# Relative-position bias of an attention layer: from mirrored distances in DRAM to full rows written into SBUF

## The chip, the cores and the metric

The kernel runs on one core of a Trainium2 chip. The metric is the device time of one execution in microseconds (us). TensorE's engines are called PE (matmuls) and PEld (weight loads), VectorE is DVE, ScalarE is ACT, GpSimd is POOL, and SP issues the DMAs.

## The reference

An attention layer, a dense feed-forward layer and a soft mixture of eight experts follow one another. Only the first is touched:

```python
B, H, S, D = q.shape                                   # 4, 8, 576, 64
scores = scale * np.matmul(q, k.transpose(0, 1, 3, 2))
psi_rel = np.log1p(np.abs(pos[:, None] - pos[None, :]))
psi_i = np.log1p(np.maximum(pos[:, None], 1.0))
x = (psi_rel / psi_i)[..., None]                       # one number per (query, key)
h = np.maximum(x @ w1 + b1, 0.0)                       # 32 hidden units
bias = h @ w2                                          # one bias per head
scores = scores + bias.transpose(2, 0, 1)[None]        # the same for the four batches
attn = softmax(scores); out = attn @ v
```

For a given query the bias is a function of the distance |i - j| alone. A hidden unit is on or off on either side of one distance, since x grows with the distance. So the bias of a pair is x times a sum of w1 w2 over the units that are on, plus a sum of b1 w2 over the same units; the units that are on are a mask of zeros and ones.

## The kernel before

**Bias phase** (`bias_phase`, lines 74 to 261). A mask tile holds 128 rows, 4 keys (distances) times 32 hidden units, and one column per query. `make_mask` (line 139) makes mask t of 144 by comparing the queries' positions `pr` with a threshold `wl` per row, on DVE, POOL or ACT as the table ENGS says (ACT as a very steep sigmoid). Sixteen masks are a key group k, of 64 distances; there are nine. Since only distances are needed, and query i has none beyond max(i, 575 - i), queries are paired from the middle outwards (ROWS, line 1249): the masks of group k have min(576, 128 (9 - k)) columns. `unit(k, c)` (line 153) takes 128 of these columns, as the weights of 48 matmuls of 64 moving columns (line 165): three bf16 parts of the products w1 w2 and b1 w2 for eight heads. There are 30 such units, and five of 64 columns for the middle queries (c = 4), taken two and two. DVE then multiplies by x (line 189) and adds (line 190) into `rows`; POOL writes the same values backwards beside them (line 198). When a chunk of distances is complete, `flush` writes it to the DRAM tensor W (line 203), in which each query has a row of 1152 with the distances to the left and to the right.

**Attention** (class `Attention`, from line 264). 16 pairs of (two heads, batch) have 9 steps each, 144 steps; a step is 128 queries of one head (one step of the nine: the last 64 of both), in the order SLOT. `scores` makes the products in PSUM, `shift` (line 397) adds the bias from the tile `nb` and takes the row's extreme, giving `z`; `weights` (line 416) takes the exponential, `transposes` and `gather` (lines 433, 457) turn it, `pv` (line 472) multiplies by v. The bias of two heads, 128 x 9 x 576 f32, is read from W by `bias_rows` (line 310) with a shifted start in every row, just before the first of the four batches that use it. `split` (lines 345, 348) divides q and k into two parts on POOL. The results go to DRAM as `xT` and `rs` and come back for the feed-forward layer. While the attention runs, DVE also puts together the first weights of the next layer (`half_piece`, lines 641 to 644, from the tile `early`, loaded at line 622).

**Order.** The instructions of each engine are ordered by a planner that simulates the kernel; those that the code marks with `keep_in_program_order` (the attention from pair 1 on, `half_piece`, some DMAs) stay in the order of the code. Each engine takes its instructions strictly in that order; all DMAs of this phase go through SP's queue. PSUM has four accumulators for the bias phase; the attention's tiles take their place. Tiles in SBUF are laid out in stacks from both ends; a tile that lies where an earlier one lay waits until that one has been read for the last time.

Of the kernel before, what the change touches and what calls it, by code (L numbers as in the profile page):

```python
# [35 lines left out]
NG = 9  # L36
NTQ = S // 4
PITCH = 2 * S
RING = 40
ACC = 4  # L40
CHUNKS = ((0, 2, 4, 7, 9), (0, 2, 4, 6, 8), (0, 3, 5, 7), (0, 2, 4, 6), (0, 2, 4, 5))
TAGS = ("cfgc", "becb", "gbd", "ada", "mnm")
LATE, EARLY = "bcdg", "aefmn"
ENGS = (
    "VVVVAAVVVVAVVVVV", "VPAVAVAAAAAAAAVV", "PAAVAVPAAAAAAAVA", "AAAAVVAVVPAAAAAA", "AAAAPAAVPVAPPVAV", "AVAAAPAVAAAVPPAV",
    "AAAAAVVVAAPAAAAA", "PPAAVVAAAVPAVAAA", "APAPPVPVAAAPAAVA",
)
# [26 lines left out]
def bias_phase(tc, ident, W, cpack, lcol, prow, xmain, xtail, att):  # L74
# [3 lines left out]
    with ExitStack() as ctx:  # L78
# [4 lines left out]
        fps = {tag: p for p, tags in ((pool("b_late"), LATE), (pool("b_rows"), EARLY)) for tag in tags}  # L83
        cp = pool("b_const")
        mp = pool("b_mask")
        ap_ = ctx.enter_context(tc.tile_pool(name="b_acc", bufs=ACC, space=PSUM, reuse_waits="tile"))
# [3 lines left out]
        wl = cp.tile([P, NTQ], F32, name="wl")  # L90
        nc.sync.dma_start(wl, lcol)
        pr = cp.tile([P, S], F16, name="pr")
        nc.sync.dma_start(pr, prow)
        xm_t = cp.tile([P, NG, 4, 64], F32, name="xm_t")
        xt_t = cp.tile([P, 3, 64], F32, name="xt_t")
        nc.sync.dma_start(xm_t[:, 0], xmain[:, 0])
# [7 lines left out]
        sg = cp.tile([P, 4], F32, name="sg")  # L104
        nc.scalar.activation(sg[:, 3:4], ident[:, :1], AF.Exp)

# [32 lines left out]
        def make_mask(k, u):  # L139

            t = 16 * k + u
            n = min(S, 128 * (NG - k))
            dst = mask[:, t % RING, :n]
            on = ENGS[k][u]
            if on == "A":
                nc.scalar.activation(dst, pr[:, :n], AF.Sigmoid, bias=wb[:, t : t + 1], scale=BIG)  # L146
            else:
                eng = nc.vector if on == "V" else nc.gpsimd
                eng.tensor_scalar(dst, pr[:, :n], wl[:, t : t + 1], None, ALU.is_gt)

        rows, accs, late = {}, {}, []

        def unit(k, c):

            if c < 4 or k % 2 == 0:
                accs[c] = ap_.tile([P, 2, 2, H, 32], F32, tag="acc", name=f"acc{k}_{c}")
            acc = accs[c]
            if c < 4:
                m, cols, dst = P, slice(P * c, P * c + P), acc
            else:  # L160
                m, cols = 64 * (k % 2) + 64, slice(512, S)
                dst = acc[m - 64 : m]
            for u in range(16):
                for part in range(3):
                    nc.tensor.matmul(  # L165
                        dst[:, u // 8, :, :, 4 * (u % 8) : 4 * (u % 8) + 4],
                        mask[:, (16 * k + u) % RING, cols],
                        wp[:, part],
                        start=part == 0,
                        stop=part == 2,  # L170
                    )
            if c == 4 and k in (0, 2):
                return
            ks = CHUNKS[c]
            i = max(n for n in range(len(ks)) if ks[n] <= k)
            d0, w, f0 = 64 * ks[i], 64 * (ks[i + 1] - ks[i]), 64 * (k - ks[i])
            last = k + 1 == ks[i + 1]
            if c == 4:
                w, f0, xs = 64, 0, xt_t[:m, i]
            else:  # L180
                xs = xm_t[:, k, c]
            if f0 == 0:
                tag = TAGS[c][i]
                rows[c] = fps[tag].tile([P, H, 2 * w], F32, tag=tag, name=f"rows{c}_{i}")
            both = rows[c]
            fwd = both[:m, :, w + f0 : w + f0 + 64]
            tmp = cp.tile([P, 2, H, 32], F32, tag="tmp", name=f"tmp{k}_{c}", bufs=2)
            xb = xs.rearrange("p (s j) -> p s j", s=2).unsqueeze(2).to_broadcast([m, 2, H, 32])
            nc.vector.tensor_tensor(tmp[:m], acc[:m, :, 0], xb, ALU.mult)
            nc.vector.tensor_tensor(fwd.rearrange("p h (s j) -> p s h j", s=2), tmp[:m], acc[:m, :, 1], ALU.add)  # L190

            one = d0 == 0 and c < 4
            z = int(one and f0 == 0)
            a = both[:m, :, w + one - f0 - 64 : w + one - f0 - z]
            back = bass.AP(
                tensor=a.tensor, offset=a.offset + 63 - z, ap=[list(v) for v in a.ap[:2]] + [[-1, 64 - z]]
            )
            nc.gpsimd.tensor_scalar(back, fwd[:, :, z:], 1.0, 1.0, ALU.mult, ALU.mult)
            if not last:
                return  # L200

            def send(dst, src, pin):
                i = nc.sync.dma_start(dst, src)
                if pin:
                    tc.keep_in_program_order(i)

            def put(half, blk, d0, n_r, n_l, one, hs):

                q = slice(64 * half, 64 * half + 64)
                dst = W[blk if blk >= 4 else 3 - blk, hs].rearrange("h p j -> p h j")  # L210
                if one:
                    send(dst[:, :, S - n_l : S - 1 + n_r], both[q, hs, w - n_l + 1 : w + n_r], hs.start > 0)
                    return
                if n_r > 0:
                    send(dst[:, :, S - 1 + d0 : S - 1 + d0 + n_r], both[q, hs, w : w + n_r], hs.start > 0)
                if n_l > 0:
                    y = int(d0 == 0)
                    send(dst[:, :, S - d0 - n_l : S - d0 - y], both[q, hs, w - n_l : w - y], hs.start > 0)

            def flush(hs):  # L220
                if c == 4:
                    for half in range(m // 64):
                        put(half, 4, d0 + 64 * half, 64, 64, False, hs)
                else:
                    far, near = min(w, S - 64 * c - d0), max(0, min(w, 64 * c + 64 - d0))
                    put(0, c, d0, far, near, one, hs)
                    put(1, 8 - c, d0, near, far, one, hs)

            if c < 3 and (k + 1 == ks[-1] or c == 0 and i == 2):
                flush(slice(0, 2))  # L230
                late.append(lambda: flush(slice(2, H)))
            else:
                flush(slice(0, H))
# [3 lines left out]
        nc.sync.dma_start(xt_t, xtail)  # L237
        for k in range(1, NG):
            nc.sync.dma_start(xm_t[:, k], xmain[:, k])
        att.load(0)  # L240
        for k in range(NG):
            cs = [c for c in range(3, -1, -1) if k <= NG - 1 - c]
            if k < 5:
                cs.append(4)
            done = 0
            for n_, c in enumerate(cs):
                unit(k, c)
                if c in (2, 3) and k + c == 8:
                    att.bias_first(3 - c)
                if k + 1 < NG:  # L250
                    upto = 16 * (n_ + 1) // len(cs)
# [3 lines left out]
            if k < 4:  # L255
                att.split(0, k)
        att.load(1)
        att.bias_first(2)
        att.bias_first(3)
        for f in late:  # L260
            f()


class Attention:
# [10 lines left out]
    def __init__(self, tc, ident, W, xT, rs, qk, v_l):  # L275
        self.tc, self.nc, self.ident = tc, tc.nc, ident
        self.W, self.xT, self.rs = W, xT, rs
# [6 lines left out]
    def open_set(self, ctx, n):  # L284
        self.sets[n]["bias"] = ctx.enter_context(self.tc.tile_pool(name=f"a_bias{n}", bufs=1, reuse_waits="tile"))
# [5 lines left out]
    def bias_rows(self, hp, s, n):  # L291

        nb = self.nb[hp]
        nh = 2 if n == 1 else 1
        if s == 4:
# [18 lines left out]
    def bias_first(self, s):  # L314

        if s == 0:
            self.bias_tile(0)
# [1025 lines left out]
```

## Time and profile before

| | |
|---|---|
| time, median of 3 runs | 847.73 us (845.72 to 849.33) |
| profiled execution | 848.92 us |
| its span, first to last instruction | 847.1 us |
| PE, PEld busy | 780.9 us (92%), 641.5 us (76%) |
| DVE, ACT, POOL busy | 565.7 us, 487.7 us, 297.0 us |
| mean granted TensorE clock | 0.967 of full speed |
| HBM read, written | 91.95 MB, 21.29 MB |

The busy time of an engine is the time in which at least one of its instructions runs; matmuls are pipelined, so a busy PE isn't a PE at its peak. The bias phase lasts to about 84 us, the attention to about 323, the rest is the feed-forward layer and the experts. The 40 slices of the profile (21 us each) show PE's granted clock in tenths:

```
PE   6965699999997999999999999999999999998893
DVE  8766468889889885899434756675676556556202
PEclk9988599999999999999999999999999999999898
DMA  6799985845847321455000200230010005338995
```

A row of a view gives the line in the kernel, the engine, the operation and the tiles (written <- read), then the shape and the count. An arrow behind an idle time names what ended it.

### The profile page before, as it was taken

The page shows a single profiled execution, that of the slowest core. Times are in us where ns is not written, and L with a number is a line of the kernel's source. Part 1 is how long each engine was busy: PE and PEld are TensorE (multiplying, and loading weights), DVE is VectorE, ACT ScalarE, POOL GpSimd, SP SyncE. Part 2 cuts the span into 40 slices and gives each one's busy share as a digit, 9 for nine tenths or more (in the row PEclk, how much of TensorE's full clock was granted, in tenths as well). Part 3 has the DMA queues.
Part 4 walks back from the last instruction along what each step waited for, and adds up shares of the span by engine and source line. Part 5 has one row for each costly group of instructions (what it writes and reads, how often), then busy time and mean ns, then how long its engine had stood idle before and what let it go on. Part 6 is the DMA issues. An engine that isn't in the chain of part 4 may idle for free.

```text
span 847.1 us, 18670 instructions
## 1 busy us (share of the span) xinstructions
PE 780.9 (92%) x7444; PEld 641.5 (76%) x7444; DVE 565.7 (67%) x1058; ACT 487.7 (58%) x1066; POOL 297.0 (35%) x285
## 2 busy tenths in 40 slices
PE   6965699999997999999999999999999999998893
PEld 6965577777765776888899889888888898986341
DVE  8766468889889885899434756675676556556202
ACT  8932467787786685443445655656665656565002
POOL 6975143646463420312312241343243232131000
PEclk9988599999999999999999999999999999999898
DMA  6799985845847321455000200230010005338995
GB/s 206 176 224 199 244 199 176 215 156 151 226 126 283 108 71 60 156 199 196 29 1 0 75 1 1 79 112 10 1 29 1 1 14 185 105 119 272 403 369 225
DMA packets 59783, 114.45 MB, mean 135 GB/s; under 512 B 10672, under 2 KB 38192, under 8 KB 57904
## 3 DMA queue, kind: packets, MB, share of 16 engines
q1 hardware_dynamic: 59696, 113.26, 43.8%
q8 instruction: 58, 0.95, 0.5%
q14 instruction: 29, 0.24, 0.1%
HBM read 91.95 MB, written 21.29 MB: 134 GB/s over the span
## 4 chain that ended last, share of the span: by engine, by line
PE 38%; DMA 8%; DVE 2%; ACT 1%; issue 1%; POOL 0%; SPq 0%; DVEq 0%; ACTq 0%
PE ys L723 18%; PE h L690 17%; DMA ep<-in_mw_dram 4%; DMA em<-in_mw_dram 1%; DMA er<-in_mw_dram 1%; DMA rb<-rs 1%; DVE g L701 1%; PE lp L782 1%; DVE vv L604 1%; PE sp L842 0%; PE sp L841 0%; PE tl L829 0%; POOL w79l L679 0%; DMA vv<-xT 0%; DVE emo L1114 0%
## 5 line engine op out<-in xcount | busy, mean ns | idle before, releaser
L701 DVE SCALAR_TENSOR_TENSOR g<-g,nal 128x384 f32<-128x384 f32 x96 | 85.8, 894 | 71.9 <-ACT g L700 71.7
L416 ACT ACTIVATE e<-z,m 128x576 f32<-128x576 f32 x144 | 110.4, 766 | 4.0 <-DVE m L397 3.2
L709 ACT ACTIVATE gr<-g 128x384 fp32r<-128x384 f32 x95 | 49.7, 524 | 106.2 <-DVE g L701 106.2
L397 DVE CUSTOM_DVE_ANT_0 z<-s,nb 128x576 f32<-128x576 f32 x144 | 103.4, 749 | 10.5 <-DMA nb<-W 4.6
L433 PEld LDWEIGHTS t<-ident,e 64*128 64x128 f32 x1440 | 68.3, 143 | 47.4 <-ACT g L457 13.8
L457 ACT ACTIVATE g<-t 128x320 f32<-128x320 f32 x144 | 62.3, 432 | 61.4 <-PE t L433 46.6
L472 PE MATMUL o<-g,v 128*64 128x256 f32 (+1 forms) x640 | 95.2, 420 | 0.0
L433 PE MATMUL t<-ident,e 64*128 64x64 f32 x1440 | 81.4, 233 | 14.7 <-ACT g L457 10.8
L457 DVE COPY g<-t 128x320 f32<-128x320 f32 x144 | 69.4, 486 | 30.8 <-PE t L433 23.6
L165 PE MATMUL acc<-wp,mask 128*128 128x64 bf16 (+1 forms) x1680 | 61.0, 203 | 17.7 <-DVE rows L190 7.0
L711 DVE TENSOR_TENSOR gr<-g,gr 128x384 fp32r<-128x384 f32 x79 | 54.6, 691 | 31.6 <-ACT gr L709 30.9
L165 PEld LDWEIGHTS <-mask 128*128 128x128 bf16 (+1 forms) x1680 | 58.8, 106 | 19.8 <-issue 6.5
L379 PE MATMUL s<-kh,qh 64*128 64x288 f32 x320 | 60.5, 349 | 10.0 <-DVE rows L190 5.7
L698 ACT ACTIVATE g<-h 128x384 f32<-128x384 f32 x96 | 46.6, 485 | 37.1 <-PE h L690 35.1
L711 POOL TENSOR_TENSOR gr<-g,gr 128x384 fp32r<-128x384 f32 x16 | 19.9, 1243 | 126.1 <-ACT gr L709 119.1
L345 POOL TENSOR_SCALAR qh<-raw 128x608 fp32r<-128x608 f32 x32 | 21.8, 701 | 112.5 <-PE s L379 108.2
L472 PEld LDWEIGHTS o<-g,v 128*64 128x64 f32 x640 | 41.5, 138 | 24.9 <-issue 0.9
L146 ACT ACTIVATE mask<-pr,wb 128x576 bf16<-128x576 f16 (+4 forms) x81 | 46.9, 665 | 21.6 <-PE acc L165 21.6
L379 PE MATMUL s<-kl,qh 64*128 64x288 f32 x320 | 53.4, 306 | 0.0
L379 PE MATMUL s<-kh,ql 64*128 64x288 f32 x320 | 53.4, 306 | 0.0
L348 POOL TENSOR_TENSOR ql<-raw,qh 128x304 fp32r<-128x304 f32 x64 | 53.2, 864 | 0.0
L700 ACT ACTIVATE g<-h 128x384 f32<-128x384 f32 x96 | 46.5, 485 | 0.0
(1008 smaller groups left out, 2020.8 us busy)
## 6 DMA issues: line engine op xcount, KB each, us to landing
ep<-in_mw_dram SPq DMA_DIRECT2D x30, 512.0 KB
raw<-in_qk_dram SPq DMA_DIRECT2D x16, 896.0 KB
stage<-in_w_dram SPq DMA_DIRECT2D x14, 1024.0 KB
nb<-W SPq DMA_DIRECT2D x12, 576.0 KB
v<-in_v_l_dram SPq DMA_DIRECT2D x16, 320.0 KB
pre<-in_mw_dram SPq DMA_DIRECT2D x10, 512.0 KB
ex<-in_mw_dram SPq DMA_DIRECT2D x9, 512.0 KB
em<-in_mw_dram SPq DMA_DIRECT2D x8, 512.0 KB
```

Source lines behind the costliest of these rows:

```text
L165: nc.tensor.matmul(dst[:, u // 8, :, :, 4 * (u % 8) : 4 * (u % 8) + 4], mask[:, (16 * k + u) % RING, cols], wp[:, part], start=part == 0, ...
L348: self.nc.gpsimd.tensor_tensor(st[x, 1][:, c], src[:, c], st[x, 0][:, c].bitcast(F32), ALU.subtract)
L379: nc.tensor.matmul(s[:, hf, :288], st["q", a][d, o : o + P], st["k", b][d, 288 * h : 288 * h + 288], start=n_ == 0, stop=n_ == len(seq) - 1,),
L397: nc.vector.tensor_tensor_reduce(out=z.rearrange("p (a b) -> p a b", a=2), in0=s[:, :, :288], in1=self.nb[st["hp"]][:, self.SLOT[t]].rearr ...
L416: self.pin(i, nc.scalar.activation(e, z, AF.Exp, bias=m, scale=-1.0, accum_out=acc))
L433: self.pin(i, nc.tensor.transpose(tp[r][:, c], e[q, k0 : k0 + P], self.ident[q, q]))
L457: self.pin(i, nc.vector.tensor_copy(dst, src) if r else nc.scalar.activation(dst, src, AF.Copy))
L472: nc.tensor.matmul(o[64 * h : 64 * h + 64, :n], st["v"][:, h, c], g[:, c, :n], start=c == 0, stop=c == 4),
L690: nc.tensor.matmul(h, w_[:, c * P : (c + 1) * P], x_[:, c], start=c == 0 and n_ == 0, stop=c == NC - 1 and n_ == 2,)
L701: nc.vector.scalar_tensor_tensor(g, neg, self.nal[:, f : f + 1], g, ALU.mult, ALU.add)
L711: eng.tensor_tensor(gl, g, gh.bitcast(F32), ALU.subtract)
L723: i = self.nc.tensor.matmul(self.ys[blk][t], g_[:, t * P : (t + 1) * P], w_[:, 512:], start=f == 0 and n_ == 0, stop=f == NF - 1 and n_ == 2,)
```

## The change

The masks now belong to pairs of query and key instead of query and distance, and nothing is mirrored. A row of a mask tile is a key (t times 4 plus 0 to 3) and a hidden unit; its columns are all 576 queries in natural order. Whether a unit is on depends on the query and on the distance to the key, so for each of the 128 rows a table `tab` of 1148 values is computed once from the distances (a product, an exponential, a rounding by adding and subtracting a large constant, a difference with the position); mask t compares the 576 values of `tab` that start at 572 - 4t with one threshold per row. The table is computed in two parts, first the 640 columns that the first group needs. Column 0 (query 0) is put right by a small POOL copy from `row0`. All masks have 576 columns.

`unit(k, r)` takes 128 queries, and for r = 0 to 3 all nine key groups do all four: 36 units. The last 64 queries (`last_rows`) are 96 matmuls per group, with 64 weight columns and 32 moving columns, for even and odd heads into the two halves of the partitions. DVE's sum goes in three pieces into the bias tiles of heads 0 and 1, of heads 2 and 3, and into a stage for heads 4 to 7. The stage is written to the DRAM tensor `nbd` in six DMAs (four of 1.18 MB, two of 0.29) after the last group, and read back whole for the third and fourth pair of heads. The bias tiles of the first two are open from the start, and the stage replaces the `rows` tiles. The ring of masks has 32 places instead of 40; ENGS is one pattern for the first group (8 DVE, 8 ACT) and one for the others (10 ACT, 4 DVE, 2 POOL). From the diff:

```diff
-RING = 40
+WT = 4 * NTQ - 4 + S
+RING = 32
+ENGS = ("VAVAVAVAVAVAVAVA",) + ("AVAAVAAPAAVAAPAV",) * 8
...
+        spread(dist[:, parts[0]], ldt[:, parts[0]], HID)
+        spread(base[:, parts[0]], brow[:, parts[0]], P)
+        spread(th, brow[:, WT:], P)
+        xt = cp.tile([P, NG, 5, 64], F32, name="xt")
+        nc.sync.dma_start(xt[:, 0], xm[:, 0])
+        spread(dist[:, parts[1]], ldt[:, parts[1]], HID)
...
-        nc.vector.tensor_scalar(wl, wl, ab, 7.0, ALU.mult, ALU.min)
-        nc.scalar.activation(wl, wl, AF.Exp)
-        nc.vector.tensor_scalar(pr, pr, sgn, None, ALU.mult)
-        nc.vector.tensor_scalar(wl, wl, sgn, None, ALU.mult)
-        nc.vector.tensor_scalar(wb, wl, -BIG, None, ALU.mult)
+        for n, c in enumerate(parts):
+            nc.vector.tensor_scalar(dist[:, c], dist[:, c], ab, 6.5, ALU.mult, ALU.min)
+            nc.scalar.activation(dist[:, c], dist[:, c], AF.Exp)
+            nc.vector.tensor_scalar(fl[:, c], dist[:, c], half, None, ALU.add)
+            nc.vector.tensor_scalar(fl[:, c], fl[:, c], half, None, ALU.subtract)
+            nc.vector.tensor_tensor(base[:, c], base[:, c], fl[:, c], ALU.subtract)
+            nc.vector.tensor_scalar(tab[:, c], base[:, c], sgn, None, ALU.mult)
...
-            n = min(S, 128 * (NG - k))
-            dst = mask[:, t % RING, :n]
+            dst = mask[:, t % RING]
+            src = tab[:, 4 * NTQ - 4 - 4 * t : 4 * NTQ - 4 - 4 * t + S]
...
+            if u == 15:
+                t0 = 16 * k
+                nc.gpsimd.tensor_scalar(
+                    mask[:, t0 % RING : t0 % RING + 16, 0], row0[:, t0 : t0 + 16], 1.0, 1.0, ALU.mult, ALU.mult
+                )
...
-            nc.vector.tensor_tensor(fwd.rearrange("p h (s j) -> p s h j", s=2), tmp[:m], acc[:m, :, 1], ALU.add)
-            nc.gpsimd.tensor_scalar(back, fwd[:, :, z:], 1.0, 1.0, ALU.mult, ALU.mult)
+            nc.vector.tensor_tensor(tmp, acc[:, :, 0], xs.unsqueeze(2).to_broadcast([P, 2, H, 32]), ALU.mult)
+            for dst, h in (
+                (nbs[0][:, r : r + 6 : 5, c], slice(0, 2)),
+                (nbs[1][:, r : r + 6 : 5, c], slice(2, 4)),
+                (stage[:, :, r, c], slice(4, 8)),
+            ):
+                nc.vector.tensor_tensor(
+                    dst.rearrange("p t (s j) -> p s t j", s=2), tmp[:, :, h], acc[:, :, 1, h], ALU.add
+                )
+        def last_rows(k):
...
+                    for q in range(2):
+                        rhs = wp[:, part].rearrange("p (a h g) -> p a h g", a=2, h=H)[:, :, q::2]
+                        dst = acc[64 * q : 64 * q + 64, kk, :, :, 4 * u : 4 * u + 4]
+                        nc.tensor.matmul(dst, lhs, rhs, start=part == 0, stop=part == 2)
...
+            for n_, r in enumerate((1, 2, 3, 4, 0)):
+                if r < 4:
+                    unit(k, r)
+                else:
+                    last_rows(k)
...
+            if 2 <= k < 6:
+                att.split(0, k - 2)
+            if k == 2:
+                att.load(1)
+        for q in range(2):
+            dst = nbd[q].rearrange("p (t n) -> p t n", t=9)
+            for par in range(2):
+                nc.sync.dma_start(dst[:, 5 * par : 5 * par + 4], stage[:, 2 * q + par])
+            nc.sync.dma_start(dst[:, 4], stage4[:, q])
...
-        if b == 0 and hp > 0:
-            self.bias_tile(hp)
-            self.bias_rows(hp, 0, 4)
-            self.bias_rows(hp, 4, 1)
+        if b == 0 and hp > 1:
+            t = self.bias_tile(hp)
+            nc.sync.dma_start(t.rearrange("p t n -> p (t n)"), self.nbd[hp - 2])
...
+    att.open_set(rctx, 1, side="right")
+    for hp in range(2):
+        att.bias_tile(hp)
...
-ROWS = [64 * blk + r for blk in (3, 5, 2, 6, 1, 7, 0, 8, 4) for r in range(64)]
+ROWS = list(range(S))
```

## Rows read from the trace of the kernel before

**Rows 1.** Busy us by stretch (from:to, length, each engine, clock, DMA)

```profile
16.00:38.00 22.00, 21.90 (x706) 21.43 (x704) 21.43 (x36) 21.33 (x33) 22.00 (x30) 1.00 0.53 145
38.00:84.00 46.00, 29.84 (x818) 28.69 (x817) 27.35 (x49) 14.99 (x33) 30.59 (x42) 0.86 1.00 214
84.00:121.00 37.00, 28.84 (x287) 22.12 (x289) 19.49 (x51) 17.96 (x45) 8.10 (x12) 0.72 1.00 236
121.00:323.00 202.00, 191.22 (x2694) 143.07 (x2692) 177.13 (x453) 156.81 (x432) 94.50 (x119) 0.98 0.55 163
```

**Rows 2.** Waits from 38 to 122 us: total us, times, longest

```profile
DVE rows L190 <- DMA W<-rows: 14.0, 4, 6.1
ACT g L457 <- DMA W<-rows: 6.0, 1, 6.0
DVE z L397 <- DMA nb<-W: 4.6, 2, 2.3
```

**Rows 3.** Starts of z on DVE, first scores on PE: start us, us, instruction

```profile
84.43 0.61 PE L379 MATMUL s<-kh,qh 64*128 64x288 f32 x2 [5.72 <-DVE rows L190]
85.55 0.76 DVE L397 CUSTOM_DVE_ANT_0 z<-s,nb 128x576 f32<-128x576 f32 x1 [0.68 <-PE s L379]
120.83 0.76 DVE L397 CUSTOM_DVE_ANT_0 z<-s,nb 128x576 f32<-128x576 f32 x1
139.57 0.75 DVE L397 CUSTOM_DVE_ANT_0 z<-s,nb 128x576 f32<-128x576 f32 x1
```

**Rows 4.** Groups by shape up to 115 us: busy us, mean ns, idle before

```profile
L165 PE MATMUL acc<-wp,mask 128*128 128x64 bf16 x1440 | 53.0, 204 | 16.8 <-DVE rows L190 6.1 <-DVE mask L149 5.9 <-issue 3.9
L165 PE MATMUL acc<-wp,mask 128*64 128x64 bf16 x240 | 8.5, 196 | 0.9 <-DVE rows L190 0.9
L146 ACT ACTIVATE mask<-pr,wb 128x576 bf16<-128x576 f16 x43 | 28.9, 760 | 0.6 <-PE acc L165 0.6
L190 DVE TENSOR_TENSOR rows<-tmp,acc 128x512 f32<-128x512 f32 x32 | 21.2, 680 | 14.3 <-DMA W<-rows 14.0
L189 DVE TENSOR_TENSOR tmp<-acc,xm_t 128x512 f32<-128x512 f32 x30 | 20.0, 681 | 4.9 <-PE acc L165 4.7
L149 DVE TENSOR_SCALAR mask<-pr,wl 128x576 bf16<-128x576 f16 x29 | 14.6, 563 | 0.1
L149 POOL TENSOR_SCALAR mask<-pr,wl 128x576 bf16<-128x576 f16 x8 | 14.0, 1757 | 0.0
```

**Rows 5.** Line 165 alone, 28 to 30 us: PE and PEld

```profile
28.00:30.00 2.00, 2.00 (x75) 2.00 (x72) 1.00 0.44 108
```

**Rows 6.** Groups by shape on DVE, whole span: two small forms

```profile
L1050 DVE COPY gst<-turn 128x256 f32<-128x256 f32 x2 | 0.8, 425 | 4.2 <-ACT gst L1048 4.2
L884 DVE TENSOR_TENSOR cs<-c,cs 128x128 f32<-128x128 f32 x1 | 0.3, 293 | 0.0
```

**Rows 7.** DVE in order of time, one unit and the next

```profile
28.81 0.68 DVE L189 TENSOR_TENSOR tmp<-acc,xm_t 128x512 f32<-128x512 f32 x1
29.52 0.69 DVE L190 TENSOR_TENSOR rows<-tmp,acc 128x512 f32<-128x512 f32 x1
30.12 0.68 DVE L189 TENSOR_TENSOR tmp<-acc,xm_t 128x512 f32<-128x512 f32 x1
```

**Rows 8.** SP and DVE in order of time at the start

```profile
1.19 0.42 SPq L91 DMA_DIRECT2D wl<-in_lcol_dram  x1
3.46 0.29 DVE L114 TENSOR_SCALAR wl<-wl,sg 128x144 f32<-128x144 f32 x1 [0.26 <-DMA wl<-in_lcol_dram]
3.88 0.37 DVE L116 TENSOR_SCALAR pr<-pr,sg 128x576 f16<-128x576 f16 x1
4.76 1.73 DVE L149 TENSOR_SCALAR mask<-pr,wl 128x576 bf16<-128x576 f16 x4
```

**Rows 9.** Busy time and DMA while the output goes out

```profile
838.00:840.00 2.00, 0.00 (x0) 0.00 (x0) 0.00 (x0) 0.00 (x0) 0.00 (x0) 0.70 1.04 395
```

**Rows 10.** DVE in order of time, first reader of early

```profile
117.57 0.42 DVE L641 TENSOR_SCALAR wr<-early 128x512 uint32<-128x512 uint32 x1
```

More of the change, by code (lines that the diff above doesn't have):

```diff
@@ L89, in bias_phase, with spread @@
         nc.sync.dma_start(cp_t, cpack)
[L90 to L96, printed above, removed]
+        stage = sp.tile([P, 4, 4, S], F32, name="stage")
+        stage4 = sp.tile([P, 2, S], F32, name="stage4")
+        flat = stage.rearrange("p h t n -> p (h t n)")
+        dist, base, fl = flat[:, :WT], flat[:, WT : 2 * WT], flat[:, 2 * WT : 3 * WT]
+        th = cp.tile([P, NTQ], F32, name="th")
+        cut = WT - 640
+        parts = slice(cut, WT), slice(0, cut)
+        def spread(dst, src, n):
+            dims = [list(v) for v in src.ap]
+            nc.sync.dma_start(dst, bass.AP(tensor=src.tensor, offset=src.offset, ap=[dims[0], [0, n], dims[1]]))
+        spread(dist[:, parts[0]], ldt[:, parts[0]], HID)
[4 more added lines that the diff above has]
+        spread(dist[:, parts[1]], ldt[:, parts[1]], HID)
+        spread(base[:, parts[1]], brow[:, parts[1]], P)
+        nc.sync.dma_start(xt[:, 1:], xm[:, 1:])
         w1_t, b1_t, de_t = cp_t[:, 0:1], cp_t[:, 1:2], cp_t[:, 10:14]
@@ L104, in bias_phase @@
         sg = cp.tile([P, 4], F32, name="sg")
+        tab = cp.tile([P, WT], F16, name="tab")
+        row0 = cp.tile([P, NTQ], BF16, name="row0")
+        th0 = cp.tile([P, NTQ], F32, name="th0")
         nc.scalar.activation(sg[:, 3:4], ident[:, :1], AF.Exp)
@@ L163, in unit @@
+        nbs = att.nb
+        mid = {}
+        def unit(k, r):
+            acc = ap_.tile([P, 2, 2, H, 32], F32, tag="acc", name=f"acc{k}_{r}")
             for u in range(16):
+                lhs = mask[:, (16 * k + u) % RING, P * r : P * r + P]
+                dst = acc[:, u // 8, :, :, 4 * (u % 8) : 4 * (u % 8) + 4]
                 for part in range(3):
[L165 to L171, printed above, removed]
@@ L172, in unit @@
-            if c == 4 and k in (0, 2):
-                return
[L174 to L184, printed above, removed]
@@ L194, in unit @@
[L194 to L197, printed above, removed]
-            nc.gpsimd.tensor_scalar(back, fwd[:, :, z:], 1.0, 1.0, ALU.mult, ALU.mult)
[L199 to L233, printed above, removed]
+                    nc.tensor.matmul(dst, lhs, wp[:, part], start=part == 0, stop=part == 2)
@@ new lines, in last_rows @@
+        def last_rows(k):
+            kk = k % 2
+            if kk == 0:
+                mid[0] = ap_.tile([P, 2, 2, HP, 64], F32, tag="acc", name=f"acc{k}_4")
+            acc = mid[0]
+            for u in range(16):
+                lhs = mask[:, (16 * k + u) % RING, 512:]
+                for part in range(3):
+                    for q in range(2):
+                        rhs = wp[:, part].rearrange("p (a h g) -> p a h g", a=2, h=H)[:, :, q::2]
+                        dst = acc[64 * q : 64 * q + 64, kk, :, :, 4 * u : 4 * u + 4]
+                        nc.tensor.matmul(dst, lhs, rhs, start=part == 0, stop=part == 2)
+            if kk == 0 and k + 1 < NG:
+                return
+            n = kk + 1
+            tmp = cp.tile([P, 2, HP, 64], F32, tag="tmp", name=f"tmp{k}_4", bufs=2)
+            xs = xt[:, k - kk : k + 1, 4].unsqueeze(2).to_broadcast([P, n, HP, 64])
+            nc.vector.tensor_tensor(tmp[:, :n], acc[:, :n, 0], xs, ALU.mult)
+            c = slice(64 * (k - kk), 64 * k + 64)
+            for m in range(2):
+                dst = nbs[m][:, 4, c].rearrange("p (k j) -> p k j", k=n)
+                nc.vector.tensor_tensor(dst, tmp[:, :n, m], acc[:, :n, 1, m], ALU.add)
+            dst = stage4[:, :, c].rearrange("p m (k j) -> p k m j", k=n)
+            nc.vector.tensor_tensor(dst, tmp[:, :n, 2:], acc[:, :n, 1, 2:], ALU.add)
@@ L282, in __init__, with open_set @@
         self.sets = [{}, {}]
-    def open_set(self, ctx, n):
-        self.sets[n]["bias"] = ctx.enter_context(self.tc.tile_pool(name=f"a_bias{n}", bufs=1, reuse_waits="tile"))
+    def open_set(self, ctx, n, **kw):
+        self.sets[n]["bias"] = ctx.enter_context(self.tc.tile_pool(name=f"a_bias{n}", bufs=1, reuse_waits="tile", **kw))
     def bias_tile(self, hp):
```

127 lines of the change are left out of this document (31 added, 96 removed).

## The prediction

> **What bounds the kernel now.** I read the stretches of the span first, then the waits of the stretch in which the engines fall idle, then the starts of the attention's steps. The bias phase is dense until 38 us: PE is busy 21.90 of 22 us, DVE 21.43 [rows 1]. From 38 to 84 us PE is busy 29.84 of 46 and DVE 27.35, while the DMA engines are full. The waits name the cause: DVE stands 14.0 us before writes into `rows`, because an earlier copy of that buffer has not yet left for the DRAM tensor W [rows 2]. From 84 to 121 us the attention has begun and stands again: it reads its bias back from W (DVE 4.6 us before `z`), and its tile `g` lies in memory that writes to W still hold (ACT 6.0 us). The granted clock is 0.72 there. So the first `z` starts at 85.55 us, but the seventeenth only at 120.83; the thirteen steps after it take 18.74 us, 1.44 each [rows 3]. Sixteen steps at that pace are 23 us and took 35. From 121 us on the change touches nothing that paces the steps. I therefore compare the time of the seventeenth `z` and carry the difference to the end.
>
> **What goes.** All writes to W and all reads of it, hence the 14.0 us and the stop of 84 to 121 us; the mirrored copies on POOL; the shorter masks of the later key groups.
>
> **What comes: TensorE.** Today there are 1680 matmuls, 1440 with 128 mask columns and 240 with 64 [rows 4]. After: 9 x 4 x 48 = 1728 of the first kind, and for the last 64 queries 9 x 16 x 3 x 2 = 864 with 64 mask columns as weights and only 32 moving columns. The dense rate is 75 in 2.00 us, 26.7 ns [rows 5]; with its small gaps 22 us hold 706 PE instructions, nearly all of them these, 31 ns. I take 28 for the 1728: 48.4 us. The 64-column kind took 8.5 us for 240, 35 ns, no less than the wide kind [rows 4]. The new kind moves half as many columns and alternates between two halves of the array, which no row shows. Bounds: 13 ns (half of the dense rate) and 35; below zero is excluded, the instructions are new. I take 30, near the row of the same weights: 25.9 us. PE sum 74 us.
>
> **VectorE.** A unit today is a product and a sum of 512 elements each; started one behind the other, a unit lasts 30.12 - 28.81 = 1.31 us [rows 7]. After, the product stays, 0.71 us until the dependent sum, and the sum is cut into 128, 128 and 256 elements for the two attention tiles and the stage. A 128-element operation lasts 0.293 us and a 256-element copy from PSUM 0.425 [rows 6]; following operations overlap by some 0.07 (0.68 long, 0.61 apart), so the sums take 0.22 + 0.22 + 0.35 = 0.79, the unit 1.50 (bounds 1.40, if small ones overlap more, and 1.69 with no overlap). There are 36 units and 5 of the last rows (two key groups each, one of them alone): 41 x 1.50 = 61.5 us, where today 33 x 1.31 are 43 us. Masks on DVE: 32 after the first group at 0.50 (14.6 us for 29, with POOL working beside it [rows 4]): 16.0 us. Bounds 0.42 and 0.563 each. Eight masks of the first group 3.4 us; the second part of the table and `row0`, some six operations, 2.2 us. DVE sum 83.1 us, so DVE, not PE, is now the slower of the two. In the dense stretch it was busy 97.4% [rows 1]: 85.3 us.
>
> **ScalarE and POOL.** ACT makes 88 masks; 43 took 28.9 us, 0.67 each [rows 4]: 59 us, hidden. POOL's 16 masks at 1.76 are 28 us; its splits are today's, its mirrored copies go and nine small copies of column 0 come: hidden under 85. That POOL slows the DVE masks is held in the 0.50.
>
> **The start.** Before, DVE waits for `wl` until 3.46 us and the first mask starts at 4.76 [rows 8]. Now the distances (128 x 640 f32, 328 KB) come first. `wl`, 72 KB, landed 2.3 us after its issue at 1.19 [rows 8]; 256 KB more at about 400 GB/s [rows 9] add 0.65: landed at 4.2. Then a product, an Exp, an add, a subtract, a two-tensor subtract and a product to f16, each waiting for the last: 0.45, 0.85, 0.42, 0.42, 0.77 and 0.42, scaled from 144 and 512 elements [rows 4, 7, 8], with hand-overs 3.8 us. First mask at 8.0, 3.2 later than now; bound 4 earlier or later with the landing. The distance load replicates four rows of DRAM. By the Trainium skill, "DMA: Bandwidth & Descriptors", section on why a DMA increments its semaphore by 16, the count of DMA engines follows the slowest dimension of both sides, here four: an estimate by that page is four engines instead of sixteen, so 3.3 us of transfer instead of 0.8. No row here shows a load with so short a first dimension; by it the result would be 2.5 us higher than mine.
>
> **The sum.** Last DVE operation 8.0 + 85.3 = 93.3; scores and the first `z` 1.2 us later (84.43 to 85.55 before [rows 3]) 94.5. The whole bias must be done by then, since row tile 0 is last and step 0 needs it. Sixteen more steps: 23 us at 1.44, 1 less because the first four are scored ahead: seventeenth `z` at 116.5, against 120.83.
>
> One thing is late next. The stage (41 KB per partition) takes the place in memory where later `early` lies; its 5.3 MB go out only when the last key group is done. At 395 GB/s, the rate of rows of 2 KB going out at the end [rows 9], 13.4 us; with landing, and then 512 KB into `early`, 18 us after the first `z`. The first pinned DVE operation that reads `early` stands in the step behind the sixteenth `z` (117.57 before [rows 10]), 19 to 20 us after the first. I charge 0.5 us. Behind it on DVE is the whole attention; behind the load of `early` on SP's queue stand the stores of xT, which nothing reads for some steps yet, and I cost them at nothing. If the writes go at the 236 GB/s of the W traffic [rows 1], it is 9 us more.
>
> Gain 4.3 - 0.5 = 3.8 us. The profiled execution took 848.92 us, so 845.1; it lay 1.2 above the median of the runs, 847.73, so I expect a median of 844. One measurement of this kernel tells 0.5%, 4.2 us, from no change; the forecast is just inside that.
>
> **Rivals.**
> 1. The bias phase is quicker. For it: the 128x64 matmuls were already at 26.7 ns, two array halves may run side by side, and POOL, with the copies gone, may slow DVE masks less. DVE at 1.40 per unit and 0.42 per mask is 57.4 + 13.4 + 5.6 = 76.4, 78.4 us with idle time: 7 us earlier, 837. Against: POOL keeps 28 us of masks beside its splits.
> 2. TensorE sets the pace and the kernel is slower. Place: the 864 matmuls, each with a weight load of its own. DVE's 85.3 us is passed when one costs over (85.3 - 48.4) / 864 = 43 ns, and the gain is eaten at 47. At one and a half times the row, 53 ns, PE needs 94.2 us, 9 more: 853. For it: no row has 32 moving columns with switching halves, and 64-column weights were no cheaper than 128. Against: 35 ns measured. The Trainium skill, "TensorE: Matmul & The Clock Gate", section LDWEIGHTS, has a load cost its columns divided by 1.2 GHz, 53 ns for 64, and faster loads only at 128 columns; the 35 ns of rows 4 speak against it.
> 3. The stage holds `early` and with it DVE (9 us): 852. For it: the same kind of wait stands in rows 2 for `g`. Against: 9 KB rows instead of pieces under 2 KB.
> 4. The change gives nothing because the stop of 84 to 121 us was hidden: the pace after it excludes that, and it gets no chance of its own.
>
> **Chances.** Forecast 0.42, its own range 840 to 848. Rival 1 0.28, rival 2 (with a start 4 us later or a poor order of DVE's queue, which end in the same place) 0.20, rival 3 0.10. Faster by over 0.5%: rival 1 and the lower third of the forecast, 0.42. Slower: most of 2 and 3, 0.24. The same: 0.34. Range 835 to 854.
>
> **What would show it.** Right: no wait for W anywhere; DVE over 95% busy from about 15 us to the first `z`; that `z` at 90 to 98 us, the seventeenth 21 to 23 us behind; granted clock 1.00 up to there. Wrong: PE without gaps in the bias phase while DVE idles (rival 2); a DVE wait on `early` or the stage's writes (rival 3); a first mask after 11 us; a different pace of the later steps.

## The result: 1.3% slower, and the profile after

The changed kernel takes 858.78 us (median of 4 runs, 856.46 to 863.37), the kernel before 848.22 beside it (4 runs): ratio 1.0135, 95% interval 1.0109 to 1.0161. The forecast was 844, in a range of 835 to 854. The profiled execution of the changed kernel took 863.37 us, the longest of its four; its span is 861.6.

What the change takes out did go: no engine waits for W any more, and from the first `z` on there is no stop for the bias. But the bias phase, which before ended in fits and starts, now begins late and is held up in its middle. Busy time of each engine by stretch (from:to, length, busy us with the number of instructions in the order PE, PEld, DVE, ACT, POOL, then granted clock, DMA share and GB/s), changed kernel, against [rows 1]:

```profile
0.00:16.00 16.00, 0.00 (x0) 0.00 (x0) 2.86 (x9) 2.33 (x4) 4.34 (x17) 1.00 0.74 203
16.00:38.00 22.00, 16.64 (x528) 15.73 (x528) 20.71 (x52) 20.56 (x30) 16.90 (x19) 1.00 0.40 150
38.00:60.00 22.00, 17.95 (x588) 17.36 (x588) 17.29 (x46) 14.45 (x22) 11.74 (x13) 0.85 0.14 45
60.00:84.00 24.00, 22.56 (x865) 22.06 (x866) 22.20 (x66) 19.42 (x30) 11.54 (x9) 1.00 0.02 5
84.00:100.00 16.00, 13.86 (x520) 13.45 (x517) 13.65 (x38) 8.04 (x11) 4.76 (x8) 1.00 0.02 4
110.00:121.00 11.00, 10.86 (x128) 8.67 (x124) 8.27 (x24) 8.39 (x22) 0.00 (x0) 0.86 0.67 273
```

TensorE (first busy column) does nothing in the first 16 us, where the kernel before had started its masks at 4.76 us [rows 8]; it stands idle for another 9 us between 16 and 60, 2 of them still the start. Only from 60 to 84 us is the phase dense. VectorE (third column) is not above 94% busy in any of these stretches.

The start, VectorE in order of time (start, length, line, operation; in brackets what it waited for), against [rows 8]:

```profile
8.96 0.55 DVE L129 TENSOR_SCALAR stage<-stage,sg 128x640 f32<-128x640 f32 x1 [6.00 <-DMA stage<-in_ldt_dram]
...
10.84 0.56 DVE L132 TENSOR_SCALAR stage<-stage 128x640 f32<-128x640 f32 x1
15.38 0.48 DVE L129 TENSOR_SCALAR stage<-stage,sg 128x508 f32<-128x508 f32 x1 [3.98 <-DMA stage<-in_ldt_dram]
15.78 0.82 DVE L133 TENSOR_TENSOR stage<-stage 128x640 f32<-128x640 f32 x1
...
17.69 1.48 DVE L172 TENSOR_SCALAR mask<-tab,th 128x576 bf16<-128x576 f16 x5
```

The first operation on the distances starts at 8.96 us, where the forecast had them landed at 4.2. Then the queue order costs a second wait: the first operation of the table's second part (508 elements) stands ahead of the last operations of its first part, and so the first masks wait 3.98 us for distances that they do not need. First mask at 17.69 us, forecast 8.0.

The steps of the attention, first and seventeenth `z` and the operations between the sixteenth and it, against [rows 3]:

```profile
105.85 0.76 DVE L357 CUSTOM_DVE_ANT_0 z<-s,nb 128x576 f32<-128x576 f32 x1 [0.95 <-issue]
...
126.49 0.76 DVE L357 CUSTOM_DVE_ANT_0 z<-s,nb 128x576 f32<-128x576 f32 x1
...
127.93 0.52 DVE L600 TENSOR_SCALAR wr<-early 128x512 uint32<-128x512 uint32 x1
130.19 0.49 DVE L440 COPY xo<-o 128x320 f32<-128x320 f32 x1 [1.74 <-PE o L432]
...
131.20 0.76 DVE L357 CUSTOM_DVE_ANT_0 z<-s,nb 128x576 f32<-128x576 f32 x1
149.94 0.75 DVE L357 CUSTOM_DVE_ANT_0 z<-s,nb 128x576 f32<-128x576 f32 x1
```

The seventeenth is 10.37 us later than before, the thirtieth too (139.57 before); the medians differ by 10.56. So most of what the change does to the time is there by 131 us. Not all of it in these two executions: their times differ by 14.45 us, and 2.3 of the remaining 4.1 come between the seventeenth `z` and the last (335.55 against 322.89).

Groups of instructions by shape up to 121 us (busy us, mean ns of one, idle before them and its causes), against [rows 4]:

```profile
L190 PE MATMUL acc<-wp,mask 128*128 128x64 bf16 x1728 | 58.6, 198 | 28.0 <-DVE mask L172 18.1 <-issue 4.8 <-POOL mask L175 3.5
L172 POOL TENSOR_SCALAR mask<-tab,th 128x576 bf16<-128x576 f16 x16 | 28.2, 1771 | 21.7 <-PE acc L190 12.1 <-DVE tab L134 9.5
L193 DVE TENSOR_TENSOR tmp<-acc,xt 128x512 f32<-128x512 f32 x36 | 24.6, 686 | 5.9 <-PE acc L190 5.6
L172 DVE TENSOR_SCALAR mask<-tab,th 128x576 bf16<-128x576 f16 x40 | 18.2, 491 | 3.8 <-PE acc L190 3.7
L200 DVE TENSOR_TENSOR nb<-tmp,acc 128x128 f32<-128x128 f32 x72 | 17.3, 282 | 0.7
L216 PE MATMUL acc<-wp,mask 128*64 128x32 bf16 x864 | 16.4, 184 | 1.7 <-issue 1.7
L200 DVE TENSOR_TENSOR stage<-tmp,acc 128x256 f32<-128x256 f32 x36 | 14.9, 414 | 0.0
```

PE's largest wait inside the phase is 3.5 us for POOL. It is a copy of column 0, which needs 0.26 us and stands in POOL's queue behind the splits of `q` and `k`. POOL in order of time:

```profile
32.11 1.63 POOL L308 TENSOR_TENSOR kl<-raw,kh 128x288 fp32r<-128x288 f32 x2
33.73 3.42 POOL L172 TENSOR_SCALAR mask<-tab,th 128x576 bf16<-128x576 f16 x2
37.12 2.39 POOL L308 TENSOR_TENSOR ql<-raw,qh 128x304 fp32r<-128x304 f32 x3
39.49 0.26 POOL L175 TENSOR_SCALAR mask<-row 128x16 bf16<-128x16 bf16 x1
```

PE, in the same form, from 34.8 us on:

```profile
34.83 1.49 PE L216 MATMUL acc<-wp,mask 128*64 128x32 bf16 x84
39.81 8.01 PE L190 MATMUL acc<-wp,mask 128*128 128x64 bf16 x192 [3.50 <-POOL mask L175]
```

PE stops at 36.3 us and goes on at 39.81. Behind the stop the granted clock is 0.50 from 40 to 44 us (1.2 instead of 2.4 GHz), and 192 wide matmuls take 8.01 us, where a dense stretch has 203 in 6.06 (76 to 84 us).

### The profile page after: what moved, and what is told of

Same layout as the page of the kernel before. It is cut to its first block, busy times and chain, and to the rows that moved or that the text cites. A ratio compares the mean times of both kernels' runs of the same rounds, so it can differ in the third digit from the quotient of the medians.

```text
span 861.6 us, 20457 instructions
## 1 busy us (share of the span) xinstructions
PE 792.0 (92%) x8356; PEld 651.8 (76%) x8356; DVE 583.0 (68%) x1160; ACT 501.1 (58%) x1074; POOL 282.9 (33%) x260
## 5 line engine op out<-in xcount | busy, mean ns | idle before, releaser
L190 PE MATMUL acc<-wp,mask 128*128 128x64 bf16 x1728 | 58.6, 198 | 28.0 <-DVE mask L172 18.1
L190 PEld LDWEIGHTS <-mask 128*128 128x128 bf16 x1728 | 56.1, 102 | 29.5 <-DVE mask L172 18.1
L169 ACT ACTIVATE mask<-tab,wb 128x576 bf16<-128x576 f16 x88 | 59.4, 761 | 12.6 <-PE acc L190 12.6
```

What stands on the lines that cost most here:

```text
L169: nc.scalar.activation(dst, src, AF.Sigmoid, bias=wb[:, t : t + 1], scale=BIG)
L190: nc.tensor.matmul(dst, lhs, wp[:, part], start=part == 0, stop=part == 2)
```

## Experiments

Theory S: the loss is at the start (slow load, then a wait in VectorE's queue). Rival B: the start does not matter, since the phase gives an early start back further on. Later theory Q came in: the rest is POOL's queue. Each ratio is to the kernel before, run beside it.

**e1_rows: the load alone.** The distances lie in DRAM once for each of the 128 partitions, and a plain load brings them; the order of the instructions is that of the changed kernel, but for one piece of a split that POOL takes between two masks instead of behind them.

```
+ ldt = np.repeat(ldt, HID, axis=0)
- spread(dist[:, parts[0]], ldt[:, parts[0]], HID)
+ nc.sync.dma_start(dist[:, parts[0]], ldt[:, parts[0]])    # and parts[1] likewise
```

> The distances reach DRAM already repeated, 128 rows instead of 4, and are loaded row for row; the order of all engines' instructions is the same as in the changed kernel. Theory S (the late start of the first mask, 17.69 us instead of the forecast 8.0, is the whole miss, and comes from the load of four rows running on few DMA engines, share 0.21 to 0.30 from 3 to 5 us): the first distances land at about 4.4 us instead of 8.9, the second part before 8 instead of 15.4, the first mask starts at 9 to 10, and the total falls by about 8 us, to 851. Rival B (the bias phase is paced by its own middle, and an earlier start is given back there): first mask as early, total within 2 us of 859. Rival Q (the loads are slow through their bytes or the re-reading, not the number of engines): first mask not before 15, total 859.

Measured: 851.46 us, ratio 1.0041 (1.0009 to 1.0073). VectorE at the start:

```profile
4.07 0.55 DVE L129 TENSOR_SCALAR stage<-stage,sg 128x640 f32<-128x640 f32 x1 [1.01 <-DMA stage<-in_ldt_dram]
...
8.70 0.48 DVE L129 TENSOR_SCALAR stage<-stage,sg 128x508 f32<-128x508 f32 x1 [2.25 <-DMA stage<-in_ldt_dram]
...
11.01 1.20 DVE L172 TENSOR_SCALAR mask<-tab,th 128x576 bf16<-128x576 f16 x4
```

The first mask comes 6.7 us earlier, the first `z` (96.95) 8.9, the seventeenth (121.59) 9.6, the median 7.3. So the load is the larger part of the loss. The DMA share says how it differs. From 3 to 4 and 4 to 5 us, changed kernel, then e1_rows from 3 to 4:

```profile
3.00:4.00 1.00, 0.00 (x0) 0.00 (x0) 0.00 (x0) 0.00 (x0) 0.80 (x3) 1.00 0.21 82
4.00:5.00 1.00, 0.00 (x0) 0.00 (x0) 0.00 (x0) 0.00 (x0) 0.55 (x2) 1.00 0.30 113
```

```profile
3.00:4.00 1.00, 0.00 (x0) 0.00 (x0) 0.06 (x1) 0.00 (x0) 0.83 (x4) 1.00 0.93 297
```

A share of 0.21 to 0.30 is about four of the 16 DMA engines; with 128 rows it is 0.93.

**e2_order and e3_both: VectorE's order.** The second part of the table is held behind the first group's masks on VectorE; e2 with the four-row load, e3 with that of e1.

```
+ table(parts[0], True); ... first group's masks (kept in order) ...; table(parts[1], True); column(0)
```

> The load of four rows stays; DVE's work on the second part of the table is put behind the first group's masks, in a fixed order, so that the first mask no longer waits for the second load (DVE stood 4.0 us before it). Theory S: first mask at about 12.7 us instead of 17.7, total 5 us less, about 854. Rival B: total within 2 us of 859.

> Both edits. Theory S: first mask at about 8.2 us, near the forecast 8.0, total 9.5 us less than the changed kernel, about 849.5, so level with the kernel before. Rival B: 857 to 859.

Measured: e2 857.37, ratio 1.0128 (1.0082 to 1.0174), e3 851.6, ratio 1.0069 (1.0047 to 1.0091): nothing gained over the changed kernel and e1, although the first mask came at 12.83 and 8.55 us. For VectorE's order B was right (e3 lies between the two forecasts, level with e1), and ScalarE's queue in e3 shows why:

```profile
9.64 6.10 ACT L168 ACTIVATE mask<-tab,wb 128x576 bf16<-128x576 f16 x9
15.76 1.28 ACT L132 ACT_TABLE_LOAD   x1
17.05 0.63 ACT L132 ACTIVATE stage<-stage 128x508 f32<-128x508 f32 x1
17.70 1.28 ACT L168 ACT_TABLE_LOAD   x1
23.36 6.10 ACT L168 ACTIVATE mask<-tab,wb 128x576 bf16<-128x576 f16 x9 [4.38 <-DVE tab L136]
```

The Exp of the second part now stands behind nine masks, with a table load of 1.28 us on either side, and the copies of column 0 and the second group's masks wait for it: PE stops 4.5 us from 20 us on (in e2 6.6 us before 29.74).

**e4_col: e3 with the column copies on ScalarE.**

```
- nc.gpsimd.tensor_scalar(mask[:, t0 % RING : t0 % RING + 16, 0], row0[...], 1.0, 1.0, ...)
+ nc.scalar.activation(mask[:, t0 % RING : t0 % RING + 16, 0], row0[...], AF.Copy)
```

> As the kernel with both edits, and the copies of column 0 go from POOL, where one stood behind the splits of q and k and held PE for 3.5 us, to ACT. Theory S with a second term (these copies cost 3.5 us and the fall of the granted clock behind them some 2 more): 844 to 846, the granted clock 1.00 through the bias phase. Rival: another wait takes the place (the copy on ACT behind its ten masks), total as with both edits alone, 849 to 850.

Measured: 850.32, ratio 1.0043 (1.0021 to 1.0065), first `z` 98.44. The stop of e3 stays, and no gain over e3 is told apart.

**e5_four to e8_ring.** In e5 each part of the distances comes in four loads, one DRAM row into 32 partitions each; DRAM keeps its four rows. e6 is e5 with the copies on ScalarE; on top of e6, e7 moves 16 masks from VectorE to ScalarE, and e8 has RING = 48.

```
+ for g in range(4):
+     spread(dist[HID * g : HID * g + HID, c], ldt[g : g + 1, c], HID)
```

> As the changed kernel, but each part of the distance load is cut into four loads, each of one DRAM row into 32 partitions; the DRAM tensor stays 4 rows. Theory S (a load whose slowest dimension is 4 runs on 4 DMA engines; with 32 it runs on all 16): as e1_rows, the first operation on the distances starts at 4.1 to 4.6 us, first mask at 11 to 11.5, first z at 97, time 851.5 (850 to 853). Rival R (reading one DRAM row 32 times is itself slow, whatever the number of engines; e1_rows was quick since its rows were laid out in DRAM): distances land after 7 us, first mask after 15, time 856 or more.

> e5_four, and the copies of column 0 run on ScalarE instead of POOL, where they stood behind the splits. Theory P (TensorE's stop of 3.7 us for that copy and the half clock after it are on the path to the first z): the stop at 33 to 37 us is gone, 192 wide matmuls there take 5.2 us instead of 7.3, the first z comes 3 to 6 us earlier than in e5_four, time 846 to 849. Rival D (VectorE's own queue sets the first z, TensorE would have waited for it anyway): the stop goes, but the first z moves by less than 1 us and the time by less than 1.5 us.

> e6_col with 16 of VectorE's 40 masks given to ScalarE (VectorE 24, ScalarE 104, POOL 16): 7.3 us less work on VectorE, 10.7 more on ScalarE (70 us of it in all). Theory D (VectorE paces the bias phase, as the prediction had it): the first z 5 to 7 us earlier than in e6_col, time 5 us less. Theory T (TensorE paces it: 58.6 + 16.4 us of matmuls in some 85 us, VectorE's waits for it take up what is saved): the first z within 1.5 us, the time within 1.5 us of e6_col.

> e6_col with 48 places for masks instead of 32, so that mask engines may run a whole key group farther ahead. If the engines' waits for a free place (ScalarE 12.6 us, POOL 12.1, VectorE 3.7 in the changed kernel) delay TensorE, the first z comes 2 to 4 us earlier and the time falls by as much; if the masks always stand ready before TensorE wants them, both stay within 1 us of e6_col.

Measured: 855.44 (1.0051 to 1.0158), 853.87 (1.0054 to 1.0119), 856.46 (1.0086 to 1.0136), 856.69 (1.0094 to 1.0167). The first mask came at 9.6 to 9.8 us in all four, ahead of e1's 11.0. The product on the distances starts at 5.58 in e5: later than S had it (4.1 to 4.6), because four issues on SP take 2.52 us, but 1.9 us behind the last of them, and not after 7 as R had it. For the load S held. But the median expected of e5 failed by 4 us. The new loads had changed the planned order, and the second Exp again stood behind nine masks. In e5 POOL then took twelve pieces of the splits ahead of its first mask (28.91 us). PE in e5 is the first busy column:

```profile
20.00:28.00 8.00, 1.85 (x59) 1.54 (x58) 7.89 (x16) 3.70 (x7) 8.00 (x10) 0.75 0.37 125
28.00:36.00 8.00, 4.75 (x111) 4.61 (x112) 2.80 (x5) 5.19 (x8) 8.00 (x10) 0.50 0.27 109
```

POOL is busy throughout, VectorE until 28 us, PE is not: it waits 4.35 us for a mask of VectorE and 3.0 for that mask of POOL. Neither the copies on ScalarE nor fewer masks on VectorE nor more places cured it: e6 to e8 stand at 1.85 to 2.49 us of PE in 20 to 28 us too. With that stop ahead of it none of them tells what sets the pace; e10 and e11 ask it of a kernel without the stop.

**e9_late: e1 with POOL's queue in order.** Masks and column copies in the order of the groups, the splits of the first two pairs behind the masks of groups 4 to 8.

```
+ tc.keep_in_program_order(i)   # POOL's masks, its column copies, the splits of pairs 0 and 1
...
- if 2 <= k < 6: att.split(0, k - 2)
+ if 3 <= k < 7: att.split(0, k - 3)
+ if 4 <= k < 8: att.split(1, k - 4)
...
- for k in range(4): self.split(1, k)      # at the start of the attention
```

> e1_rows, with POOL's queue in an order written out: its masks and copies of column 0 in the order of the groups, the splits of q and k for the first two attention pairs (18 us of POOL) behind the masks of groups 4 to 8 instead of in front of those of group 2. Theory Q (what e1_rows, e5_four and e6_col lose between 20 and 44 us is POOL's queue, in which the splits stand ahead of masks and copies that TensorE needs): no stop of TensorE for POOL of over 1 us, granted clock 1.00 throughout, first z 4 to 6 us after e1_rows' less, so 91 to 93 us, time 845 to 848. Rival D (VectorE's own work sets the first z): the stop goes, the first z stays within 1.5 us of 97.

Measured: 846.42 (10 runs), ratio 1.0000 (0.9982 to 1.0018), first `z` 93.50, seventeenth 116.85. Three stretches of e9, then the second of them in e1_rows:

```profile
20.00:28.00 8.00, 7.55 (x289) 7.25 (x284) 7.90 (x26) 8.00 (x13) 4.89 (x4) 1.00 0.02 5
28.00:36.00 8.00, 7.72 (x313) 7.54 (x308) 7.83 (x24) 8.00 (x13) 3.85 (x4) 1.00 0.02 4
36.00:44.00 8.00, 7.75 (x312) 7.55 (x308) 7.45 (x24) 8.00 (x13) 3.84 (x3) 1.00 0.03 7
```

```profile
28.00:36.00 8.00, 4.05 (x122) 3.89 (x117) 5.64 (x14) 5.38 (x9) 8.00 (x11) 0.83 0.34 117
```

In 28 to 36 us, where e1_rows had PE at 4.05 us and a clock of 0.83, PE is now busy 7.72, no wait for POOL is left, and the clock is full. Q held: 5.0 us from e1 by the medians, 3.5 by the first `z`, which came half a microsecond behind the range expected. (The planner also changed the order of some masks and sums on VectorE.)

**e12_pool: POOL's order alone**, with the four-row load.

> The changed kernel with only POOL's order of e9_late written out; the distance load stays the four-row one. Theory A (the slow load and POOL's queue each cost their own part, one behind the other): first mask 17.7 as in the changed kernel, first z 82 to 83 us behind it, so 100 to 101, against 105.85; time 853 to 855. Rival O (the late start hides POOL's queue or the other way round, so that e9_late needed both): first z within 1.5 us of 105.85 or as early as 97, time 858 or 849.

Measured: 855.59, ratio 1.0089 (1.0057 to 1.0121). VectorE's masks up to 30 us (shortest, median and longest in ns, then the starts of the first and the last), and the first `z`:

```profile
L172 DVE TENSOR_SCALAR mask<-tab,th x15: 362/366/369, 17.5 to 29.2; 128x576 bf16<-128x576 f16 x15
...
99.15 0.76 DVE L366 CUSTOM_DVE_ANT_0 z<-s,nb 128x576 f32<-128x576 f32 x1 [0.95 <-issue]
```

First mask and first `z` are 81.7 us apart, where the changed kernel needs 88.2. Theory A holds for the phase; the median is 0.6 us above the range expected, and the profiled run (852.04) was the fastest of four. By the ratios the load is worth 0.94%, POOL's order 0.46% and both 1.35%; the intervals of the changed kernel and of e12 still touch, so the smaller share rests on the trace and on e1 to e9.

**e10_fewer and e11_acts: what paces the phase once nothing stops it.** e10 is e9 with 288 instead of 864 narrow matmuls: it leaves out two of the three parts of the products for the last 64 queries. e11 is e9 with 16 masks moved from VectorE to ScalarE.

```
- for part in range(3):                       # last_rows, e10
+ for part in range(1):
- ENGS = ... + ("AVAAVAAPAAVAAPAV",) * 8      # e11
+ ENGS = ... + ("AAAVAAAPAAVAAPAA",) * 8
```

> e9_late without two of the three parts of the matmuls for the last 64 queries: 288 of 64x32 instead of 864, 10.7 us less on TensorE at 18.5 ns each (the last queries' bias is then that of the first part alone). If TensorE's work paces the dense part of the bias phase: first z 8 to 10 us earlier than in e9_late. If VectorE's units and masks pace it: less than 2 us earlier.

> e9_late with 16 of VectorE's masks on ScalarE (7.3 us less on VectorE). If VectorE paces the dense part: first z 5 to 7 us earlier than in e9_late, time 5 us less. If TensorE paces it, or ScalarE now does (70 us of masks between 11 and 85): within 1.5 us.

Measured: e10 841.46, ratio 0.9944 (0.9923 to 0.9966), first `z` 87.61; e11 844.71, ratio 0.9987 (0.9965 to 1.0010), first `z` 94.74. From 44 to 76 us, one fence each for e9, e10 and e11:

```profile
44.00:76.00 32.00, 28.71 (x1078) 27.75 (x1073) 30.77 (x85) 26.17 (x40) 27.15 (x28) 1.00 0.11 33
```

```profile
44.00:76.00 32.00, 26.13 (x875) 24.82 (x872) 31.93 (x88) 28.41 (x42) 27.97 (x31) 1.00 0.09 32
```

```profile
44.00:76.00 32.00, 29.16 (x1117) 28.29 (x1118) 28.34 (x80) 32.00 (x49) 24.24 (x27) 1.00 0.02 5
```

10.7 us less on TensorE bring the first `z` 5.9 us nearer, and then VectorE is full (31.93 of 32). So TensorE sets the end of the phase by some 6 us, with VectorE close behind it: between the two expectations for e10. In e11, 7.3 us less on VectorE bring nothing; its waits for TensorE before the products grow instead, from 6.1 to 13.4 us. By itself e11 doesn't settle it: ScalarE is full there (32.00 of 32) and finishes its last mask at 81.6 us, where e9 does at 77.3, so that ScalarE may have kept back a gain; this rival was not tested.

What remains open is 6.7 us of PE's idle time in e9, in pieces of up to 1.1 us for which the profile names no cause ("issue"). The trace says where they stand: from 31.84 to 88.91 us each lies 127 to 128 or 255 to 256 matmuls behind the one before it, and from 30 to 92 us the instruction queue moved 16 packets of 16 KB, one for every 128 of the 2041 matmuls. That points to the supply of instructions and not to another engine's work; it was not tested.

**e13_part and e14_both: a version that beats both?** e9 with the first part of the table finished before VectorE waits for the second, and that with e11's masks.

```
+ keep = tc.keep_in_program_order   # round every table operation on VectorE and both Exp; first group's ScalarE masks too
```

> e9_late with the first part of the table finished on VectorE before it waits for the second part's distances (a wait of 2.0 us goes), ScalarE's first masks kept behind the second Exp as far as the planner lets them. If the start still passes through to the end: first mask at 8.6 to 9.2 instead of 11.2, first z 91 to 92 instead of 93.5, time 1.5 to 2.5 us below e9_late. If the second part, needed for the copies of column 0 and the later masks, now sets the start: TensorE stands for VectorE or ScalarE masks between 10 and 25 us, first z within 1 us of e9_late, or later.

> e13_part with 16 of VectorE's masks on ScalarE, as in e11_acts. TensorE sets the pace there, so no more than 1.5 us to either side of e13_part.

Measured: 847.31, ratio 1.0008 (0.9988 to 1.0028), and 845.81, ratio 0.9986 (0.9963 to 1.0009). The first mask of e13 came at 9.11 us, but one ScalarE mask (9.38 us) slipped ahead of the second Exp, which then had a table load before and behind it (10.17 and 12.11 us), PE waited 3.7 us for a ScalarE mask, and the first `z` (93.08) is where e9 has it. Here an earlier start was worth nothing, since the second part did not follow it. In e14 the first `z` is at 95.55. Of the kernels that do the whole work none came out faster than the kernel before; only e10, which leaves a part out, did.

## Why the prediction was wrong

Against the forecast the seventeenth `z` is 14.7 us late (131.20 against 116.5), and the median 14.8. By the steps:

- **The step that failed is "The start": "landed at 4.2", "first mask at 8.0".** The first mask came at 17.69, 9.7 us late and outside the 4 us allowed for the landing. The landing was scaled from `wl` and a rate of 400 GB/s, as if every load used all DMA engines; this one ran at a share of 0.21 to 0.30 and landed at 8.96. e1_rows has the first product at 4.07, as forecast, once the slowest dimension is 128, and e5_four at 5.58 with 32 and four issues. Behind that I counted only the chain of the first part (3.8 us) and not what stands between in VectorE's queue: the second part's product, with a wait of 3.98 us of its own. Without both, in e13, the chain from the first product (4.10) to the finished first part (7.99) takes 3.9 us: it was sized right. The estimate by the Trainium skill ("DMA: Bandwidth & Descriptors", section on why a DMA increments its semaphore by 16) pointed the right way: four engines. Its 2.5 us were half of the 4.8 us by which the landing was late. What made the other half was not separated; from 5 to 9 us, with the loads issued behind it under way, the DMA share is 0.88 to 1.14.
- **"POOL ... hidden under 85" failed too, under a total that came out near by luck.** First mask to first `z` took 88.2 us, forecast 86.5. But the forecast was VectorE's 85.3 us with hardly a gap. VectorE had only 75.67 us of work from 17.7 to 105, 87% of that time, and the rest went to waits: TensorE stood for POOL's queue and then ran at half clock. With POOL's order mended it is 81.7 (e12) and 82.3 (e9). Only busy sums were compared for POOL, never the place of a 0.26 us copy behind 11.5 us of splits (both pairs' splits take 14 us; the 18 in e9's expectation were too many).
- **"DVE, not PE, is now the slower of the two" was wrong**, as e10 shows. TensorE's sum was close, 73.66 us from 17.7 to 105 against 74: the wide matmuls take 30 ns in the dense part (203 in 6.06 us at 76 to 84 us), not 28, the narrow ones less than forecast. VectorE's sum, 83.1, was 7.4 too high: its masks take 0.455 us each, not 0.50, a unit 1.45 back to back (products at 88.09, 89.54 and 90.99 us), not 1.50, and part of the table's second half was done before the first mask. So the 76.4 us of rival 1 are what VectorE really had to do, but its time of 837 did not come, because the start was late and VectorE waited.
- **Rival 2 is refuted in its place:** the 864 narrow matmuls took 19 ns each, 16.4 us, below the 30 I took. Its other ending, "a start 4 us later or a poor order", is what came (the start 9.7 us late, and the poor order on POOL besides DVE), and I had put it in a bracket at a price too low.
- **The ramp of 22 us was 25.35.** Between the sixteenth and seventeenth `z` stand the first reader of `early` and a wait for the first `o`: 4.71 us, and the kernel before has the same 4.70 there (116.13 to 120.83). I counted it as a step of 1.44: 3.3 us missed in a row that could be read.
- **Rival 3 is refuted:** the loads of `early` were issued from 119.95 us on, behind the stage's writes, their data moved until about 126, and the first reader at 127.93 did not wait; the 0.5 us charged were not needed.
- **The carry was right** for the changed kernel: 10.37 us at the seventeenth `z`, 10.56 in the median, though the profiled executions lie 14.45 apart. It was poorer for e9: seventeenth `z` 4.0 us earlier than before, median the same, and its profiled run (843.95 us) was the fastest of its ten. From the seventeenth to the last `z` 202.06 us pass before and 202.4 to 207.8 in the kernels after, with granted clocks of 0.98 to 0.96. Why the later attention differs by so much was not tried.
- **Two readings were off** by less than 0.1 us, which changes nothing: following operations start 0.60 apart in [rows 7], not 0.61, and the first `z` starts 1.12 us behind its scores in [rows 3], not 1.2.

Of the signs named in advance, the first mask after 11 us came, and the signs of being right did not: VectorE was 87% busy instead of 95, and the granted clock fell to 0.85 in 38 to 60 us. The missing wait for W came as said.

So the expected gain was there: the stop of 84 to 121 us is gone, and that pays for a bias phase with more work, but only just. The load and POOL's order then cost 11.4 us on top (0.0135 x 847).

## What to carry to other kernels

Size a load by the engines that it can use, as well as by its bytes: where a few DRAM rows are replicated over partitions, lay them out row by row in DRAM (e1) or cut the load (e5), and look at the DMA share in the first microseconds. When work is moved onto an engine whose busy sum has room, look for what stands ahead of each small operation in its queue; a copy of 0.26 us behind splits stopped TensorE for 3.5 us, and behind the stop its granted clock was 0.50 for 4 us. And when a stall at the start is mended, follow the second thing that the same stage waits for, or the gain can be handed back a few microseconds later, as in e2 and e3.

## What was not expected of the hardware

- Matmuls with 64 weight columns and 32 moving columns, alternating between two column halves, ran at 19 ns each (16.4 us for 864), where the wide kind with 128 weight columns and 64 moving ones needs 30.
- While the load that replicates 4 rows of DRAM into 128 partitions ran (3 to 5 us), the DMA moved 82 to 113 GB/s; with 128 rows in DRAM it moved 297 in the first of these.
- VectorE's masks took from 0.35 to 0.99 us in one kernel (mean 0.455). In e5 one at 25.25 us lasts 0.90 while POOL makes a split, and a 128x508 product at 23.38 lasts 1.10 instead of 0.48; that POOL is the cause was seen side by side and not tested.
- TensorE's pauses without a named cause lie 127 to 128 or 255 to 256 matmuls apart (e9), one packet of 16 KB of the instruction queue for every 128; they cost it 6.7 us of the phase.
